# A softmax over the state: DVE's 32x32 block transposes in place of TensorE's

## Chip, cores and metric

The kernel runs on one core of one Trainium2 chip. The metric is the device time of one execution in microseconds, median of the runs. Engines are named as in the profile: PE (TensorE), DVE (VectorE), ACT (ScalarE), POOL (GpSimd), SP (the queue that issues the DMAs).

## What is computed

An attention of 512 tokens and 32 state rows in both directions for 4 batches and 8 heads of width 64, and behind it two feed-forward layers over all 2,176 rows:

```python
scores = scale * x @ state.T            # 512 x 32 for each batch and head
a = softmax(scores, axis=-1)            # over the 32 state rows
xread = a @ state
a2 = softmax(scores.T, axis=-1)         # over the 512 tokens
sread = a2 @ x
h = concat([xread, sread]) as rows of 512
h = prelu(h @ w_in, alpha) @ w_out      # 512 -> 2048 -> 512
out = softplus(h @ moe2_w_in) @ moe2_w_out
```

The change is in `a`, the softmax over the state.

## The kernel before, in words

Every large product is made of three fp32r matmuls (`mm3`, lines 140 to 142): a tile is split into a high half (`split`, line 146, on ACT) and a low half (line 149, on DVE or POOL), and high x high, low x high and high x low are added in PSUM. The weights come as 8-byte words and are converted tile by tile (`wconv`): ACT runs lines 206 and 207, DVE lines 208 to 210, POOL line 211, and the names `exp` and `top` are one buffer each. `wprep` converts and splits the next tile.

The attention works in eight groups: group i holds batch i // 2 and four of its heads. `at_load_t` brings x transposed into scratch tiles t[0] and t[1], `at_load_x` brings x as it is into t[2] and t[3]. Three sets of six scratch tiles take turns, so group 3 uses group 0's (t[0] is acc_94, t[1] is acc_95). For a group:

- `at_scores` (lines 265 to 279) multiplies state by x into one PSUM bank: on the partitions 4 heads x 32 state rows, along the free axis 512 tokens. ACT copies it to t[4] (line 274), DVE takes the maximum (275), ACT takes exp with its sum into t[5] (277).
- `at_rows` (281 to 296) transposes t[4] by four PE transposes of 128x128 (line 287) into another bank, so that tokens lie on the partitions and 16 runs of 32 state rows along the free axis. DVE takes the maximum of each run (290) and subtracts it on the way to t[1] (291), ACT takes exp (292), DVE sums (293) and inverts, POOL multiplies (296).
- `at_back` (298 to 304) transposes t[1] back by four more PE transposes (303) into a bank and splits it into the tiles `at` (high on ACT, low on DVE).
- `at_read` (306 to 334) makes `sread` from t[5], and uses t[0] for a small tile on the way; ACT's line 334 copies its result out of PSUM.

`sw_batch` (line 242) multiplies state by the first layer's weights, so that `hidden` of the first layer multiplies `at` by `sw`. `hidden` (line 348) makes a hidden block in a bank, `act` applies the activation (lines 379 and 383 in the first layer), `out_part` multiplies by the second weights with a lag of three blocks.

PSUM has two pools of four banks, `psa` and `psb`. `pool_s` (line 450) gives the attention's banks from the two in turns, counted over its calls, for the first five groups, and from `psa` after that; `hidden` and `sw_batch` take from `psa`. A bank is given out again when its last reader is done.

Two things set the order of the work. The strings BEFORE and AMONG (lines 47 and 48) set the order in which the steps are written: s, r, d and b are the scores, rows, read and back of a group, x and y its loads, c and p conversions, w a `sw_batch`. A scheduler then sets the order on each engine's queue from its own model of the durations; on the chip each queue runs in that order. Tiles that the order below names pa_... and pb_... are banks.

Of the kernel before, what the change touches and what calls it, by code (L numbers as in the profile page):

```python
# [14 lines left out]
AF = mybir.ActivationFunctionType  # L15
# [43 lines left out]
def mixer_kernel(  # L59
# [200 lines left out]
    def scratch(i):  # L260
        for x in sets[i % 3]:
            held.pop(x.name, None)
        return [x.f for x in sets[i % 3]]

    def at_scores(i):

        b, g = i // 2, i % 2
        t, n2 = scratch(i), st_n[i % 3]
        ps = bank(pool_s(i))
        for k in range(2):  # L270
            for hh in range(2):
                r, o = slice(hh * D, (hh + 1) * D), col(g, k, hh)
                nc.tensor.matmul(ps[o : o + NS], stf.f[r, head(2 * g + k, b)], t[k][r], start=True, stop=True)  # L273
        nc.scalar.activation(t[4], ps, AF.Copy)
        nc.vector.tensor_reduce(out=n2[:, 0:1], in_=ps, op=ALU.max, axis=AX.X)
        nc.vector.tensor_scalar(n2[:, 0:1], n2[:, 0:1], -SCALE, None, op0=ALU.mult)
        nc.scalar.activation(t[5], ps, AF.Exp, bias=n2[:, 0:1], scale=SCALE, accum_out=n2[:, 1:2])
        nc.vector.tensor_scalar(n2[:, 1:2], n2[:, 1:2], EPS, None, op0=ALU.add)
        nc.vector.reciprocal(n2[:, 1:2], n2[:, 1:2])

    def at_rows(i):

        s0, e1 = scratch(i)[4], scratch(i)[1]
        m1, s1 = st_m[i % 2], st_s[i % 2]
        ps = bank(pool_s(i))
        for c in range(4):
            nc.tensor.transpose(ps[:, c * P : (c + 1) * P], s0[:, c * P : (c + 1) * P], ident)
        p3 = ps.rearrange("p (a n) -> p a n", n=NS)
        e3 = e1.rearrange("p (a n) -> p a n", n=NS)
        nc.vector.tensor_reduce(out=m1, in_=p3, op=ALU.max, axis=AX.X)  # L290
        nc.vector.tensor_tensor(out=e3, in0=p3, in1=m1.to_broadcast([P, 16, NS]), op=ALU.subtract)
        nc.scalar.activation(e1, e1, AF.Exp, scale=SCALE)
        nc.vector.tensor_reduce(out=s1, in_=e3, op=ALU.add, axis=AX.X)
        nc.vector.tensor_scalar(s1, s1, EPS, None, op0=ALU.add)
# [2 lines left out]

    def at_back(i):

        e1 = scratch(i)[1]  # L300
        ps = bank(pool_s(i))
        for c in range(4):
            nc.tensor.transpose(ps[:, c * P : (c + 1) * P], e1[:, c * P : (c + 1) * P], ident)
        split(nc.scalar, nc.vector, *R(at[i // 2][i % 2]), ps)

    def at_read(i):

# [250 lines left out]
```

## Time and profile before

| | before |
|---|---|
| median of three runs | 748.48 us (747.7 to 748.65) |
| profiled execution | 746.91 us |
| its span in the trace | 745.1 us |
| PE busy | 722.4 us, 97% |
| DVE busy | 425.2 us, 57% |
| ACT busy | 423.5 us, 57% |
| POOL busy | 170.8 us, 23% |
| DMA, mean over the span | 63 GB/s |

The span is the time between the first and the last instruction on the core; the profiled execution's own time has 1.8 us around it. Busy time is the time in which an engine has an instruction under way. PE overlaps its matmuls, and their ends are modelled, so a full PE is one that always has something to do, not one at its peak. The attention takes up the first 110 us or so, and runs there beside the first layer's first weights.

### The profile page before, as it was taken

What the parts mean: (1) busy time and instruction counts of PE and PEld (TensorE: products, weight loads), DVE (VectorE), ACT (ScalarE), POOL (GpSimd) and SP (SyncE); (2) the same over time, 40 slices, a digit from 0 to 9 for tenths busy, and PEclk for the clock granted to TensorE, in tenths of its full rate; (3) what the DMA queues carried; (4) which work ended last, traced back from release to release, by engine and by line L of the source; (5) the groups of instructions that cost most, each with busy time, mean ns of one, the idle gap of its engine ahead of it and who ended that gap; (6) DMA issues with size and microseconds to landing.
All of it is one profiled execution on the core that took longest, in us unless ns stands there. A gap on an engine that the chain in (4) does not pass through costs nothing.

```text
span 745.1 us, 9504 instructions
## 1 busy us (share of the span) xinstructions
PE 722.4 (97%) x3580; PEld 561.6 (75%) x3580; DVE 425.2 (57%) x693; ACT 423.5 (57%) x764; POOL 170.8 (23%) x142
## 2 busy tenths in 40 slices
PE   5699998999999999999999999999999999999997
PEld 2267666777778777878888888888888888888886
DVE  4898657757778456886585224664257342333433
ACT  4778767735564235564677647765466454444560
POOL 2353332412142003462572004410044000000000
PEclk9989999999999999999999999999999999999999
DMA  9654313203211001220123001220010000001102
GB/s 320 224 177 154 104 41 128 86 1 113 85 57 57 0 1 49 93 85 1 40 74 113 0 1 45 97 86 0 1 53 5 1 1 0 1 1 56 57 15 113
DMA packets 16654, 47.27 MB, mean 63 GB/s; under 512 B 2016, under 2 KB 2016, under 8 KB 16608
## 3 DMA queue, kind: packets, MB, share of 16 engines
q1 hardware_dynamic: 16608, 46.66, 18.7%
q8 instruction: 28, 0.46, 0.3%
q14 instruction: 18, 0.15, 0.1%
HBM read 42.20 MB, written 4.46 MB: 63 GB/s over the span
## 4 chain that ended last, share of the span: by engine, by line
PE 95%; DVE 2%; ACT 1%; DMA 1%; issue 0%; POOL 0%; SPq 0%; ACTq 0%
PE pb L140 17%; PE pb L141 17%; PE pb L142 17%; PE pa L140 13%; PE pa L142 12%; PE pa L141 12%; PE pa L242 2%; PE pa L363 2%; PE pa L273 1%; DMA acc<-xt 1%; DVE top L208 1%; PE pa L371 0%; PE pa L312 0%; PE pb L273 0%; ACT exp L206 0%
## 5 line engine op out<-in xcount | busy, mean ns | idle before, releaser
L390 DVE SCALAR_TENSOR_TENSOR pa<-pa,tmp 128x512 f32<-128x512 f32 x68 | 47.4, 697 | 125.7 <-ACT tmp L389 125.7
L387 ACT ACTIVATE tmp<-pa 128x512 f32<-128x512 f32 x68 | 40.6, 597 | 89.2 <-PE pa L142 69.7
L433 DVE TENSOR_TENSOR acc<-pb,acc 128x512 f32<-128x512 f32 x102 | 67.4, 685 | 35.9 <-PE pb L142 35.9
L208 DVE SCALAR_TENSOR_TENSOR top<-stg,top 128x512 uint16<-128x512 uint16 x64 | 53.0, 828 | 47.5 <-ACT top L207 46.9
L211 POOL TENSOR_TENSOR cnv<-top,cnv 128x512 f32<-128x512 bf16 x48 | 56.3, 1174 | 100.6 <-DVE cnv L210 96.8
L383 DVE SCALAR_TENSOR_TENSOR pa<-tmp,rest,pa 128x512 f32<-128x512 f32 (+1 forms) x80 | 53.2, 671 | 25.5 <-ACT tmp L379 25.0
L206 ACT ACTIVATE exp<-stg 128x512 bf16<-128x512 bf16 x64 | 43.0, 672 | 39.6 <-DVE cnv L210 28.9
L379 ACT ACTIVATE tmp<-pa 128x512 f32<-128x512 f32 x68 | 40.2, 597 | 42.2 <-PE pa L142 35.7
L207 ACT ACTIVATE top<-exp,top_bias 128x512 uint16<-128x512 uint16 x64 | 46.2, 722 | 9.3 <-POOL cnv L211 5.7
L389 ACT ACTIVATE tmp<-tmp 128x512 f32<-128x512 f32 x68 | 42.9, 631 | 1.7
L388 ACT ACTIVATE tmp<-tmp 128x512 f32<-128x512 f32 x68 | 42.9, 631 | 1.5
L210 DVE SCALAR_TENSOR_TENSOR cnv<-stg,exp 128x512 f32<-128x512 uint32 x48 | 35.8, 745 | 12.8 <-POOL wo5l L149 4.0
L209 DVE TENSOR_SCALAR exp<-top 128x512 uint16<-128x512 uint16 x64 | 32.2, 503 | 1.1
L146 ACT ACTIVATE g1h<-pa 128x512 fp32r<-128x512 f32 x33 | 19.7, 597 | 20.5 <-DVE pa L390 12.3
L146 ACT ACTIVATE g3h<-pa 128x512 fp32r<-128x512 f32 x33 | 19.7, 597 | 19.4 <-DVE pa L383 9.7
L146 ACT ACTIVATE g0h<-pa 128x512 fp32r<-128x512 f32 x33 | 19.7, 596 | 19.1 <-DVE pa L383 10.2
L149 DVE TENSOR_TENSOR g3l<-pa,g3h 128x512 fp32r<-128x512 f32 x33 | 22.7, 689 | 13.5 <-ACT g3h L146 13.2
L149 DVE TENSOR_TENSOR g1l<-pa,g1h 128x512 fp32r<-128x512 f32 x33 | 22.7, 687 | 12.6 <-ACT g1h L146 12.2
L149 DVE TENSOR_TENSOR g0l<-pa,g0h 128x512 fp32r<-128x512 f32 x33 | 22.7, 688 | 10.5 <-ACT g0h L146 10.1
L149 DVE TENSOR_TENSOR g2l<-pa,g2h 128x512 fp32r<-128x512 f32 x33 | 22.7, 686 | 10.0 <-ACT g2h L146 9.9
L146 ACT ACTIVATE g2h<-pa 128x512 fp32r<-128x512 f32 x33 | 19.8, 599 | 14.5 <-DVE pa L390 7.6
L149 POOL TENSOR_TENSOR wo3l<-cnv,wo3h 128x512 fp32r<-128x512 f32 x5 | 6.5, 1304 | 74.5 <-ACT wo3h L146 74.3
(863 smaller groups left out, 2114.5 us busy)
## 6 DMA issues: line engine op xcount, KB each, us to landing
stg<-w1i SPq DMA_DIRECT2D x16, 511.8 KB, 4.1
stg<-w1o SPq DMA_DIRECT2D x16, 511.8 KB, 3.4
stg<-w2i SPq DMA_DIRECT2D x16, 511.8 KB, 4.0
stg<-w2o SPq DMA_DIRECT2D x16, 511.8 KB, 3.3
out<-acc SPq DMA_DIRECT2D x16, 256.0 KB, 2.0
acc<-xt SPq DMA_DIRECT2D x10, 256.0 KB, 4.5
acc<-xs SPq DMA_DIRECT2D x8, 256.0 KB, 5.1
wo4h<-xt SPq DMA_DIRECT2D x3, 256.0 KB, 3.8
```

Of the source, the lines that this page charges most:

```text
L140: nc.tensor.matmul(ps, lh, rh, start=start, stop=False)
L141: nc.tensor.matmul(ps, lh, rl, start=False, stop=False)
L142: nc.tensor.matmul(ps, ll, rh, start=False, stop=stop)
L146: nc.scalar.activation(h, src, AF.Copy)
L149: eng_l.tensor_tensor(out=l, in0=src, in1=h, op=ALU.subtract)
L206: nc.scalar.activation(e, top.bitcast(BF16), AF.Abs)
L207: nc.scalar.activation(tu, eu, AF.Relu, bias=top_bias, scale=TOP_SCALE)
L208: nc.vector.scalar_tensor_tensor(out=tu, in0=top, scalar=TOP_SIGN, in1=tu, op0=ALU.bitwise_and, op1=ALU.bitwise_or)
L211: nc.gpsimd.tensor_tensor(out=a, in0=t, in1=a, op=ALU.add)
L383: nc.vector.scalar_tensor_tensor(out=ps[:, cs], in0=t[:, cs], scalar=a, in1=ps[:, cs], op0=ALU.mult, op1=ALU.add)
L390: nc.vector.scalar_tensor_tensor(out=ps, in0=ps, scalar=0.0, in1=t, op0=ALU.max, op1=ALU.add)
L433: nc.vector.tensor_tensor(out=a, in0=ps, in1=a, op=ALU.add)
```

## The change

`at_scores` no longer copies its bank to t[4]: DVE transposes it from PSUM to t[1], in blocks of 32x32. A block holds 32 state rows of one head by 32 tokens, so that after it the partitions hold 4 heads x 32 tokens and each run of 32 along the free axis holds the state rows of one token: what the maximum and the sum need. `at_rows` works in t[1]: the maximum on DVE from SBUF, the subtraction on POOL, the rest as before. `at_back` transposes t[1] by DVE into t[0] and splits that: high on ACT, low on POOL. The eight PE transposes of a group and two of its five banks go. The calls that `pool_s` counts are fewer, so the turns between the pools shift.

```diff
--- before.py
+++ after.py
@@ -271,7 +271,7 @@
             for hh in range(2):
                 r, o = slice(hh * D, (hh + 1) * D), col(g, k, hh)
                 nc.tensor.matmul(ps[o : o + NS], stf.f[r, head(2 * g + k, b)], t[k][r], start=True, stop=True)
-        nc.scalar.activation(t[4], ps, AF.Copy)
+        nc.vector.transpose(out=t[1], in_=ps)
         nc.vector.tensor_reduce(out=n2[:, 0:1], in_=ps, op=ALU.max, axis=AX.X)
         nc.vector.tensor_scalar(n2[:, 0:1], n2[:, 0:1], -SCALE, None, op0=ALU.mult)
         nc.scalar.activation(t[5], ps, AF.Exp, bias=n2[:, 0:1], scale=SCALE, accum_out=n2[:, 1:2])
@@ -280,15 +280,11 @@
 
     def at_rows(i):
 
-        s0, e1 = scratch(i)[4], scratch(i)[1]
+        e1 = scratch(i)[1]
         m1, s1 = st_m[i % 2], st_s[i % 2]
-        ps = bank(pool_s(i))
-        for c in range(4):
-            nc.tensor.transpose(ps[:, c * P : (c + 1) * P], s0[:, c * P : (c + 1) * P], ident)
-        p3 = ps.rearrange("p (a n) -> p a n", n=NS)
         e3 = e1.rearrange("p (a n) -> p a n", n=NS)
-        nc.vector.tensor_reduce(out=m1, in_=p3, op=ALU.max, axis=AX.X)
-        nc.vector.tensor_tensor(out=e3, in0=p3, in1=m1.to_broadcast([P, 16, NS]), op=ALU.subtract)
+        nc.vector.tensor_reduce(out=m1, in_=e3, op=ALU.max, axis=AX.X)
+        nc.gpsimd.tensor_tensor(out=e3, in0=e3, in1=m1.to_broadcast([P, 16, NS]), op=ALU.subtract)
         nc.scalar.activation(e1, e1, AF.Exp, scale=SCALE)
         nc.vector.tensor_reduce(out=s1, in_=e3, op=ALU.add, axis=AX.X)
         nc.vector.tensor_scalar(s1, s1, EPS, None, op0=ALU.add)
@@ -297,11 +293,9 @@
 
     def at_back(i):
 
-        e1 = scratch(i)[1]
-        ps = bank(pool_s(i))
-        for c in range(4):
-            nc.tensor.transpose(ps[:, c * P : (c + 1) * P], e1[:, c * P : (c + 1) * P], ident)
-        split(nc.scalar, nc.vector, *R(at[i // 2][i % 2]), ps)
+        t = scratch(i)
+        nc.vector.transpose(out=t[0], in_=t[1])
+        split(nc.scalar, nc.gpsimd, *R(at[i // 2][i % 2]), t[0])
 
     def at_read(i):
 
```

Since the scheduler sets the queues anew, the change also moves instructions. (Lines of the new kernel are smaller by 4 to 6 from `at_rows` on: its L287 is the subtraction, its L292 is the old L296, its L306, L312 and L322 are the old L312, L318 and L328.)

POOL, from its first weight tile on, before:

```order
L211 TENSOR_TENSOR wi0h<-top_74,wi0h 128x512
L211 TENSOR_TENSOR wi0l<-top_74,wi0l 128x512
L296 TENSOR_TENSOR acc_95<-acc_95,sts_81 128x512
L211 TENSOR_TENSOR wi1h<-top_74,wi1h 128x512
L296 TENSOR_TENSOR wo4l<-wo4l,sts_82 128x512
L211 TENSOR_TENSOR wi1l<-top_74,wi1l 128x512
L211 TENSOR_TENSOR cnv_67<-top_74,cnv_67 128x512
L149 TENSOR_TENSOR wo0l<-cnv_67,wo0h 128x512
```

Between wi0h's and wi1l's conversions stand two others and the multiplications of groups 0 and 1. With the change the same stretch of POOL's queue holds:

```order
L211 TENSOR_TENSOR wi0h<-top_74,wi0h 128x512
L287 TENSOR_TENSOR acc_95<-acc_95,stm_79 128x512
L211 TENSOR_TENSOR wi0l<-top_74,wi0l 128x512
L287 TENSOR_TENSOR wo4l<-wo4l,stm_80 128x512
L292 TENSOR_TENSOR acc_95<-acc_95,sts_81 128x512
L211 TENSOR_TENSOR wi1h<-top_74,wi1h 128x512
L292 TENSOR_TENSOR wo4l<-wo4l,sts_82 128x512
L287 TENSOR_TENSOR acc_101<-acc_101,stm_79 128x512
L149 TENSOR_TENSOR at0l<-acc_94,at0h 128x512
L211 TENSOR_TENSOR wi1l<-top_74,wi1l 128x512
L292 TENSOR_TENSOR acc_101<-acc_101,sts_81 128x512
L149 TENSOR_TENSOR at1l<-wo4h,at1h 128x512
```

The subtractions of groups 0, 1 and 2 (L287) and the low half at0l (L149) now stand in front of wi1l's conversion, and at1l two places behind it.

SP, the reloads of the first scratch set, before:

```order
L258 DMA acc_96<-xs 128x512
L258 DMA acc_97<-xs 128x512
L254 DMA acc_95<-xt 128x512
L192 DMA stg_66<-w1o 128x2047
L254 DMA acc_94<-xt 128x512
L258 DMA wo5h<-xs 128x512
```

Here the two loads of group 3 (acc_95, acc_94) stand between weight tiles. With the change the same stretch of SP's queue holds:

```order
L258 DMA acc_96<-xs 128x512
L258 DMA acc_97<-xs 128x512
L192 DMA stg_66<-w1o 128x2047
L258 DMA wo5h<-xs 128x512
L258 DMA wo5l<-xs 128x512
L254 DMA acc_95<-xt 128x512
L192 DMA stg_64<-w1o 128x2047
L254 DMA acc_94<-xt 128x512
L254 DMA wo4l<-xt 128x512
```

The loads of group 3 into acc_95 and acc_94 have moved behind two weight tiles and behind the loads of wo5h and wo5l. What was read last from acc_94 was at_read's small tile; now it is the split in `at_back`.

PE, around the first matmul of `hidden` (at0h by sw0h), before:

```order
L312 MATMUL pa_464<-ident,at7l 128x128 x4
L287 MATMUL pa_493<-ident,acc_98 128x128 x4
L140 MATMUL pa_514<-at0h,sw0h 128x512
L141 MATMUL pa_514<-at0l,sw0h 128x512
L142 MATMUL pa_514<-at0h,sw0l 128x512
L140 MATMUL pa_514<-at1h,sw1h 128x512
L141 MATMUL pa_514<-at1l,sw1h 128x512
L142 MATMUL pa_514<-at1h,sw1l 128x512
L312 MATMUL pa_534<-ident,acc_99 128x128 x4
L318 MATMUL pb_470<-acc_102,wi4l 32x64 x8
L318 MATMUL pb_470<-wi4h,wi4l 32x64 x8
```

Group 3's transposes stand directly ahead of the first `hidden` matmul, and group 2's read behind its set of six. With the change the same place on PE's queue holds:

```order
L242 MATMUL pa_416<-wi0l,ex0h 32x512
L242 MATMUL pa_417<-wi1l,ex0h 32x512
L312 MATMUL pa_447<-acc_102,wi4l 32x64 x8
L312 MATMUL pa_447<-wi4h,wi4l 32x64 x8
L140 MATMUL pa_482<-at0h,sw0h 128x512
L141 MATMUL pa_482<-at0l,sw0h 128x512
L142 MATMUL pa_482<-at0h,sw0l 128x512
L140 MATMUL pa_482<-at1h,sw1h 128x512
L141 MATMUL pa_482<-at1l,sw1h 128x512
L142 MATMUL pa_482<-at1h,sw1l 128x512
L306 MATMUL pb_502<-ident,acc_99 128x128 x4
L273 MATMUL pb_531<-wo4h,ex0h 32x512 x2
L273 MATMUL pb_531<-wo4l,ex0h 32x512 x2
```

The transposes of group 3's rows (L287) are gone from the front, and the 32 small matmuls of group 2's read (the old L318) have come to stand ahead of the first `hidden` matmul.

## Rows read from the trace of the kernel before

**Rows 1.** The page, part 1: busy time, share of the span, instructions.
```profile
PE 722.4 (97%) x3580; PEld 561.6 (75%) x3580; DVE 425.2 (57%) x693; ACT 423.5 (57%) x764; POOL 170.8 (23%) x142
```

**Rows 2.** Engines by stretch: from:to, length, PE, PEld, DVE, ACT, POOL busy, clock, DMA.
```profile
0.00:36.00 36.00, 20.70 (x167) 7.99 (x168) 23.29 (x53) 22.10 (x47) 11.00 (x15) 0.98 0.78 271
36.00:72.00 36.00, 35.86 (x294) 23.93 (x293) 33.29 (x67) 28.68 (x65) 15.41 (x14) 0.92 0.50 162
72.00:92.00 20.00, 20.00 (x132) 13.46 (x131) 14.47 (x30) 14.77 (x35) 4.93 (x5) 1.00 0.41 130
```

**Rows 3.** PE's waits, 35 to 200 us: us in total, times, longest.
```profile
PE pa L140 <- DVE g1l L149: 2.4, 1, 2.4
PE pa L140 <- DVE stn L276: 1.4, 1, 1.4
PE pa L140 <- ACT srh L334: 1.2, 1, 1.2
```

**Rows 4.** Chain that ended last, 35 to 103 us: start, length in us, what.
```profile
35.43 0.78 PE pa L140
...
43.44 0.44 PE pb L303 x4
...
89.81 0.58 PE pa L318 x32
...
92.51 0.59 ACT at6h L146
...
93.81 0.29 ACT srh L334 x2
...
102.53 0.44 PE pa L303 x4
```

**Rows 5.** Engines in stretches of 4 us; columns as in group 2 (clock behind POOL).
```profile
32.00:36.00 4.00, 1.87 (x9) 1.34 (x10) 4.00 (x11) 2.84 (x7) 1.25 (x2) 0.84 0.07 13
36.00:40.00 4.00, 4.00 (x42) 3.04 (x40) 3.88 (x10) 3.83 (x8) 2.31 (x3) 0.50 0.36 123
40.00:44.00 4.00, 4.00 (x34) 1.91 (x26) 3.96 (x8) 2.56 (x6) 2.09 (x3) 0.81 0.63 195
```

**Rows 6.** Groups, 0 to 180 us (last row: whole span): busy us, mean ns, idle before.
```profile
L291 DVE TENSOR_TENSOR acc<-pa,stm 128x512 f32<-128x512 f32 x4 | 2.7, 680 | 0.0
...
L293 DVE TENSOR_REDUCE sts<-acc 128x16 f32<-128x512 f32 x5 | 3.4, 679 | 0.0
...
L296 POOL TENSOR_TENSOR wo4l<-wo4l,sts 128x512 f32<-128x512 f32 x3 | 3.1, 1049 | 6.6 <-ACT g1h L146 5.2 <-DVE sts L295 1.4
...
L149 POOL TENSOR_TENSOR wo3l<-cnv,wo3h 128x512 fp32r<-128x512 f32 x5 | 6.5, 1304 | 74.5 <-ACT wo3h L146 74.3
```

**Rows 7.** L208 and L209, 0 to 180 us: as groups, and as minimum/median/maximum in ns.
```profile
L208 DVE SCALAR_TENSOR_TENSOR top<-stg,top 128x512 uint16<-128x512 uint16 x28 | 22.4, 801 | 20.8 <-ACT top L207 20.5
...
L209 DVE TENSOR_SCALAR exp<-top 128x512 uint16<-128x512 uint16 x28 | 9.8, 349 | 0.5
...
L208 DVE SCALAR_TENSOR_TENSOR top<-stg,top x28: 673/692/1507, 7.9 to 177.0; 128x512 uint16<-128x512 uint16 x28
...
L209 DVE TENSOR_SCALAR exp<-top x28: 276/291/1286, 8.6 to 178.2; 128x512 uint16<-128x512 uint16 x28
```

**Rows 8.** Instructions in order of time at 21.5 us: start, length, engine, what.
```profile
21.55 1.05 POOL L296 TENSOR_TENSOR wo4l<-wo4l,sts 128x512 f32<-128x512 f32 x1 [0.49 <-DVE sts L295]
...
21.85 1.29 DVE L208 SCALAR_TENSOR_TENSOR top<-stg,top 128x512 uint16<-128x512 uint16 x1 [0.47 <-ACT top L207]
```

**Rows 9.** wi1l on POOL; DMA issue (KB, us to landing); scores on the chain; L277.
```profile
24.75 1.16 POOL L211 TENSOR_TENSOR wi1l<-top,wi1l 128x512 f32<-128x512 bf16 x1 [2.15 <-DVE wi1l L210]
...
acc<-xt SPq DMA_DIRECT2D x10, 256.0 KB, 4.5
...
14.40 1.00 PE pa L273 x4
...
L277 ACT ACTIVATE acc<-pb,stn x2: 677/682/687, 11.3 to 35.8; 128x512 f32<-128x512 f32 x2
```

## Prediction

> **What bounds the kernel now.** I read the page's busy times first, then the engines by stretch, then TensorE's waits, then the chain that ended last. The page gives TensorE (PE) 97% of the span, VectorE (DVE) and ScalarE (ACT) 57% each and GpSimd (POOL) 23% [rows 1]. The stretches show that this average hides stages [rows 2]. Up to 36 us PE is busy 20.7 of 36 us: it waits for loads and for the other engines. From 36 us on it is full. From 36 to 72 us DVE is nearly full too (33.3 of 36 us, so 2.7 us idle), and from 72 us on DVE has a quarter of its time free. After 35 us PE waits only three times, 5.0 us in all [rows 3]; the first of these is in front of the first matmul of `hidden`, which starts at 35.43 us [rows 4]. So after 35.43 us what PE no longer has to do comes off the end, unless PE then waits for somebody. Before it, only the moment of that first matmul counts. One more thing lies in the start: after PE was busy 1.9 of 4 us, the granted clock falls to 0.50, the lower level of 1.2 GHz, and is still on its way back between 40 and 44 us [rows 5].
>
> **PE.** The order shows both transposing steps gone, 64 instructions in 16 groups of four. Seven of the groups stand on the chain behind 35.43 us, the first at 43.44 and the last at 102.53 us, with 0.44 us each [rows 4]: **3.1 us saved**. The rest run ahead of 35.43 us, where PE has idle time, or beside waits; I count nothing for them. The order also puts the 32 small matmuls of group 2's read in front of the first `hidden` matmul; such a set costs 0.58 us at full clock [rows 4]: **0.6 us saved** behind it.
>
> **The wait at 92 us.** There PE waits 1.2 us for a bank that ACT's L334 copies free [rows 3], and just ahead of that copy ACT splits what the transposes of group 6 left in PSUM [rows 4]. The new at_back takes no bank. I take the wait as gone: **1.2 us saved**; bounds 0 and the 3.6 us of both later waits.
>
> **DVE.** A group loses the subtraction (L291, 0.68 us) and the low half of the split from PSUM, and gains two transposes, which no row of before shows. The nearest rows are DVE's other passes over 128x512 of fp32: 0.68 us from PSUM (L291) and from SBUF (L293) [rows 6]. I take 0.69, so that the exchange costs nothing. The bounds are the cheapest and the dearest 128x512 pass of DVE, 0.28 us (16-bit data) and 1.51 us [rows 7]. By the Trainium skill, "VectorE: DVE Perf Modes", section "The three transpose paths", a 128x128 bf16 transpose takes 311 ns on DVE and 390 ns on TensorE; scaled to four such widths, an estimate from that page, one of ours would take 1.24 us on DVE, and the sum would come out 6.6 us higher. DVE's price no run here shows; on PE the trace has four transposes in 0.44 us, far less than the page.
>
> **ACT** loses eight copies (L274), which are off the path.
>
> **POOL** takes over the subtraction, in the form of L296 (1.05 us), and the low half, in the form of L149 (1.30 us) [rows 6]. That is 8 x 2.35 = 18.8 us more, and POOL was busy 26.4 of the first 72 us [rows 2]: there is room, but not at once. Two things follow.
>
> The first is a hindrance of DVE. A DVE pass of the weight conversion that starts while POOL works on two fp32 tensors is held: L208, 0.69 us alone, took 1.29 us when L296 had begun 0.30 us earlier [rows 8]. Over the first 180 us L208 averages 0.801 us for a median of 0.692, and L209 0.349 for 0.291, 28 times each [rows 7]: 28 x (0.109 + 0.058) = 4.7 us lost, with 19 such POOL passes there (8 of L296, 11 of L149): 0.25 us each. The Trainium skill, "GPSIMD Engine Reference", section "8. Key points", says that POOL shares its SBUF interfaces with DVE and contends with DVE passes in a 2-port mode or with two SBUF inputs. By that rule, and by the 1.29 us, this speaks against the change.
>
> The second is the queue. In front of the conversion of wi1l, the last tile that sw_batch needs, POOL's order has three subtractions and one low half more: 3 x 1.05 + 1.30 = 4.5 us. Most of it lies where POOL waited, but at0l stands directly in front.
>
> **The first matmul of `hidden`.** It uses the bank of group 3's scores, and these need a reload of acc_94, which now must wait for at0l on POOL. wi1l's conversion started at 24.75 us [rows 9]; I put at0l's end at 25.6, 0.9 us behind that. The reload lands 4.5 us after its issue [rows 9]: 30.1. Then come the scores 1.0 (L273) [rows 9], a transpose and two maxima, 3 x 0.69, a pass of L208, 0.69, and the exponential, 0.68 [rows 9]: 34.5. With two of the hold-ups of 0.6 us [rows 8] and some 0.7 us for small passes and hand-overs (an estimate) it is 36.4 us: **1.0 us lost**. Bounds: 2 us earlier (no hold-up, the reload early) and 3 us later. The slow clock takes half of PE's rate from 35.43 to 40 us and a fifth up to 44 us, some 3 us in all [rows 5]; I keep it as it is, and it may go or double.
>
> **DVE between 36 and 72 us.** Ten of the added POOL passes fall there: 10 x 0.25 = 2.5 us more for DVE, while PE has six groups less, 2.6 us. Against 2.7 us of idle time DVE could come up to 2.4 us late; past 72 us it has time to catch up. I take **1.0 us lost**, bounds 0 and 2.4.
>
> **Sum:** -3.1 - 0.6 - 1.2 + 1.0 + 1.0 = **-2.9 us**. The profiled execution took 746.91 us (the span of 745.1 and 1.8 us around it), so it would take 744.0. The median of the runs is 748.48 us, 1.6 above it: the forecast in those terms is **745.6 us**. About 0.2% (1.5 us) is what a measurement here can tell from no change.
>
> **Rivals.**
> 1. *Fewer banks, fewer waits.* Two bank uses a group go. If the 2.4 us wait for DVE's g1l [rows 3] and the 1.0 us of DVE's lateness go as well, the time is 745.6 - 3.4 = 742.2. For it: both late waits are for banks. Against: the second hangs on a split of DVE that stays.
> 2. *The transposes are dear and DVE becomes the bound: slower.* Six transposes stand ahead of the first `hidden` matmul and about six between there and 72 us, where DVE is the tighter engine. Each 0.1 us above 0.69 costs 1.2 us. If a transpose takes as long as a held L208, 1.29 us [rows 8], the time is 745.6 + 12 x 0.60 = 752.8; it is slower than before from 0.93 us on. For it: DVE's 33.3 of 36 us [rows 2]. Against: DVE's fp32 passes of this size show 0.68 us whatever they do. The page's 1.24 us, named above, would give 752.2.
> 3. *POOL's queue gives the gain back.* at0l, the subtractions and the conversions queue behind one another, and the first `hidden` matmul comes 3.5 us later instead of 1.0: 748.1, no change. For it: 18.8 us more on an in-order queue. Against: POOL is busy 11.0 of the first 36 us [rows 2].
> 4. *The change doesn't do what it says*: excluded by the order, which has 16 transposes on DVE and 64 fewer on PE.
>
> **How the numbers follow.** Forecast 0.51, rival 1 0.14, rival 2 0.18, rival 3 0.17. Faster by over 0.2% (below 747.0): rival 1 and most of the forecast (0.44), 0.58. Same: the rest of the forecast and most of rival 3, 0.21. Slower (above 750.0): rival 2 and a little of rival 3, 0.21. The forecast's own range is 743 to 748. To hold 8 in 10 the range takes in rival 1 with some of the clock's 3 us beyond it, and on the other side rival 3 and the nearer half of rival 2: **740.5 to 751.5 us**.
>
> **What would show it.** Right: the first `hidden` matmul at about 36.4 us; transposes of 0.65 to 0.75 us; longer means of L208 and L209 (0.9 and 0.4 us); no PE wait at 92 us. Wrong: transposes above 0.93 us; PE waits of several us for POOL (at0l, at1l, wo0l); the first matmul later than 38 us; a slow clock that lasts past 48 us.

## The result, and the profile after

The changed kernel takes **757.52 us** (median of four runs, 756.47 to 757.77), against 748.18 us for the kernel before on the same chip: 1.0122 times as long, 95% interval 1.0105 to 1.014. The forecast was 745.6 us, in a range of 740.5 to 751.5. The profiled execution took 756.47 us with a span of 754.7 us, 9.6 us more than before. Two executions among the experiments below, of 1,867.64 and 4,108.85 us, stand outside all medians here.

The page's busy times, and the first line of its chain of waits:

```profile
PE 720.7 (96%) x3516; PEld 557.5 (74%) x3516; DVE 435.3 (58%) x693; ACT 421.4 (56%) x756; POOL 192.5 (26%) x158
...
PE 86%; DVE 7%; ACT 3%; issue 2%; DMA 1%; POOL 0%; SPq 0%; DVEq 0%; ACTq 0%
```

PE has the 64 transposes less [rows 1], and is busy no longer than before; yet the span grew. So PE waited more. The engines by stretch say where (from:to, length, busy time of PE, PEld, DVE, ACT and POOL, clock, DMA):

```profile
0.00:36.00 36.00, 20.37 (x173) 6.82 (x174) 26.73 (x52) 19.74 (x40) 18.00 (x20) 0.87 0.78 270
36.00:72.00 36.00, 29.33 (x204) 18.21 (x196) 30.61 (x56) 24.89 (x55) 21.69 (x18) 0.94 0.46 139
72.00:92.00 20.00, 16.53 (x108) 10.61 (x101) 15.63 (x28) 12.02 (x30) 7.22 (x6) 0.91 0.42 140
```

From 36 to 72 us PE was full before, 35.86 of 36 us [rows 2]; now it is busy 29.33. From 72 to 92 us it falls from 20.0 to 16.53. DVE, which I had feared would be the tighter engine there, is busy *less* than before between 36 and 72 us (30.61 for 33.29): it is not full. PE's waits from 30 to 180 us name what it stood for (us in total, times, longest):

```profile
PE pa L312 <- ACT acc L307: 2.9, 1, 2.9
PE pa L312 <- ACT wo6h L307: 2.5, 1, 2.5
PE pa L140 <- DVE sw2l L149: 2.3, 1, 2.3
PE pb L140 <- ACT g0h L146: 2.1, 1, 2.1
PE pb L140 <- ACT g1h L146: 1.8, 1, 1.8
PE pa L140 <- ACT acc L277: 1.3, 1, 1.3
PE pa L273 <- DMA acc<-xt: 1.0, 1, 1.0
PE pb L140 <- ACT g2h L146: 0.8, 1, 0.8
PE pa L306 <- DVE g0l L149: 0.5, 1, 0.5
PE pb L141 <- DVE g1l L149: 0.4, 1, 0.4
```

Where before had three waits [rows 3], there are now nine behind the first `hidden` matmul and at it. The row for L277 is the first `hidden` matmul's own wait, at 37.59 us, and the DMA's 1.0 us lies ahead of it. The other eight sum to 13.3 us; before, the two behind the first matmul were 3.6 [rows 3]. The two longest are L312, the small matmuls of a read, waiting for L307, ACT's copy of that read's transposes.

**Where the 9.6 us come from.** The first `hidden` matmul starts at 37.59 instead of 35.41 us: +2.2. The waits behind it: +9.7. The granted clock falls to 0.50 twice more, behind two of the waits:

```profile
82.00:84.00 2.00, 2.00 (x6) 1.61 (x5) 1.53 (x3) 0.36 (x1) 0.32 (x2) 0.50 0.22 81
106.00:108.00 2.00, 2.00 (x6) 1.61 (x6) 0.69 (x1) 1.13 (x3) 0.79 (x1) 0.50 0.00 0
80.00:86.00 6.00, 5.60 (x46) 3.81 (x46) 3.50 (x6) 1.78 (x4) 2.71 (x3) 0.72 0.46 146
104.00:110.00 6.00, 5.35 (x16) 3.92 (x16) 2.38 (x4) 3.10 (x10) 1.53 (x2) 0.72 0.02 9
```

Over each 6 us the mean is 0.72, which loses 6 x 0.28 = 1.7 us: +3.4 for both. Not every wait is followed by a dip: behind the two longest, at 45 and 69 us, the granted clock stayed at 1.00. The dip in the start [rows 5] comes earlier now, 28 to 40 us, so that less of it lies behind the first `hidden` matmul: 1.5 us instead of 3.0 by the same sum over 2 us pieces, -1.5. Against this stands PE's saved work: ten of the groups of transposes stood behind the first `hidden` matmul before, 10 x 0.44 us, and group 2's read, 0.6: -5.0. Together 2.2 + 9.7 + 3.4 - 1.5 - 5.0 = +8.8, of the 9.6 measured.

**The first `hidden` matmul.** The chain that ended last, from DVE's conversion of wi1l through the reload of acc_94 to that matmul (start, length in us, what), and the low half at0l on POOL, behind which the prediction had put the reload:

```profile
24.79 1.02 DVE exp L209
...
25.87 1.62 DVE wi1l L210
27.54 0.33 SPq L192
...
27.96 3.57 DMA acc<-xt
...
31.67 1.08 PE pa L273 x4
...
33.66 0.72 DVE acc L274
...
34.87 0.67 DVE stm L286
35.54 1.05 DVE top L208
...
36.75 0.78 ACT acc L277 x2
```

```profile
25.62 1.31 POOL L149 TENSOR_TENSOR at0l<-acc,at0h 128x512 fp32r<-128x512 f32 x1
```

From the reload on it runs through the steps that the prediction named. Ahead of the reload it does not: at0l was done at 26.93 us, but the reload was issued only at 27.96, because the load of a weight tile (L192) stands ahead of it in SP's queue and waited for DVE's L210 on wi1l. Three held passes of DVE lie on this chain: L209 of 1.02 us, L210 of 1.62 and L208 of 1.05, where they take 0.29, 0.69 and 0.69 alone, some 2 us of hold together.

**A wait of 2.9 us, in its making.** The instructions in order of time behind 40 us, those that bear on it (start, length in us, engine, what, in brackets the idle time before it and who ended it):

```profile
40.33 1.05 POOL L292 TENSOR_TENSOR acc<-acc,sts 128x512 f32<-128x512 f32 x1 [0.70 <-ACT wo1h L146]
40.93 0.99 DVE L208 SCALAR_TENSOR_TENSOR top<-stg,top 128x512 uint16<-128x512 uint16 x1 [0.20 <-ACT top L207]
41.34 1.71 POOL L149 TENSOR_TENSOR wo1l<-cnv,wo1h 128x512 fp32r<-128x512 f32 x1
41.96 1.24 DVE L209 TENSOR_SCALAR exp<-top 128x512 uint16<-128x512 uint16 x1
43.23 0.69 DVE L210 SCALAR_TENSOR_TENSOR cnv<-stg,exp 128x512 f32<-128x512 uint32 x1
43.96 0.66 ACT L206 ACTIVATE exp<-stg 128x512 bf16<-128x512 bf16 x1 [2.31 <-DVE cnv L210]
...
44.52 0.58 ACT L307 ACTIVATE acc<-pb 128x512 f32<-128x512 f32 x1
...
45.16 0.65 PE L312 MATMUL pa<-acc,acc 128*32 128x64 f32 x32 [2.91 <-ACT acc L307]
```

POOL runs two fp32 passes back to back. DVE's L208 takes 0.99 us beside them for 0.69, and L209 1.24 for 0.29. ACT's next conversion, L206, waits 2.31 us for DVE; the copy L307, which needs nothing from DVE, stands behind L206 in ACT's queue; and PE's L312 waits 2.91 us for the copy. The two holds come to 0.30 + 0.95 = 1.25 us, so that by these rows PE would wait some 1.7 us even without them (an estimate): the place of the copy behind L206 counts as much as the lateness. PE's own queue there, from its order, with group 3's transposes and the matmuls that use their copy:

```
L306 MATMUL pb_502<-ident,acc_99 128x128 x4
L273 MATMUL pb_531<-wo4h,ex0h 32x512 x2
L273 MATMUL pb_531<-wo4l,ex0h 32x512 x2
L322 MATMUL pa_447<-ident,acc_100 128x128
L312 MATMUL pa_508<-acc_96,acc_98 32x64 x8
```

Between transposes and result stand only four score matmuls and one transpose. For group 4 it is tighter still: its L312 stands directly behind its L306, and waits 2.5 us. There ACT had its wait for DVE earlier (1.84 us, up to 64.25 us) and is busy without a gap from then on; when the transposes are done, at 66.7 us, it still has three L425 (from 66.50 us) and L207 in front of the copy, which starts at 68.55.

The new operations themselves are close to their forecast (forms of a line over 0 to 180 us: busy us, mean ns | idle before):

```profile
L208 DVE SCALAR_TENSOR_TENSOR top<-stg,top 128x512 uint16<-128x512 uint16 x26 | 21.7, 833 | 16.9 <-ACT top L207 16.8
L209 DVE TENSOR_SCALAR exp<-top 128x512 uint16<-128x512 uint16 x26 | 14.3, 551 | 0.5
L287 POOL TENSOR_TENSOR acc<-acc,stm 128x512 f32<-128x512 f32 x5 | 6.8, 1361 | 10.1 <-PE pa L306 4.5 <-DVE stn L276 3.1 <-DVE stm L286 2.5
...
L297 DVE STREAM_TRANSPOSE acc<-acc 128x512 f32<-128x512 f32 x5 | 3.4, 687 | 0.0
...
L274 DVE STREAM_TRANSPOSE acc<-pa 128x512 f32<-128x512 f32 x3 | 2.1, 711 | 0.3 <-PE pa L273 0.3
```

A transpose takes 0.69 to 0.71 us. The subtraction takes 1.05 us at the least and 1.36 on the mean of these five. L209 averages 0.551 us (0.349 before [rows 7]).

### The profile page after: what moved, and what is told of

Its sections match the earlier page's. It is cut to its first block, busy times and chain, and to the rows that moved or that the text cites. A ratio compares the mean times of both kernels' runs of the same rounds, so it can differ in the third digit from the quotient of the medians.

```text
span 754.7 us, 9368 instructions
## 1 busy us (share of the span) xinstructions
PE 720.7 (96%) x3516; PEld 557.5 (74%) x3516; DVE 435.3 (58%) x693; ACT 421.4 (56%) x756; POOL 192.5 (26%) x158
## 4 chain that ended last, share of the span: by engine, by line
PE 86%; DVE 7%; ACT 3%; issue 2%; DMA 1%; POOL 0%; SPq 0%; DVEq 0%; ACTq 0%
PE pb L141 16%; PE pb L142 16%; PE pb L140 15%; PE pa L140 12%; PE pa L142 12%; PE pa L141 12%; PE pa L357 2%; PE pa L242 2%; DMA acc<-xt 1%; DVE top L208 1%; DVE exp L209 1%; ACT exp L206 1%; ACT acc L425 1%; DVE stn L275 1%; DVE pa L377 1%
## 5 line engine op out<-in xcount | busy, mean ns | idle before, releaser
L208 DVE SCALAR_TENSOR_TENSOR top<-stg,top 128x512 uint16<-128x512 uint16 x64 | 53.7, 839 | 45.8 <-ACT top L207 45.3
L206 ACT ACTIVATE exp<-stg 128x512 bf16<-128x512 bf16 x64 | 43.0, 672 | 47.9 <-DVE cnv L210 33.5
L207 ACT ACTIVATE top<-exp,top_bias 128x512 uint16<-128x512 uint16 x64 | 46.1, 720 | 10.2 <-POOL cnv L211 5.7
L210 DVE SCALAR_TENSOR_TENSOR cnv<-stg,exp 128x512 f32<-128x512 uint32 x48 | 36.6, 763 | 12.9 <-POOL wo5l L149 4.0
L209 DVE TENSOR_SCALAR exp<-top 128x512 uint16<-128x512 uint16 x64 | 37.4, 584 | 1.2
L149 DVE TENSOR_TENSOR g3l<-pa,g3h 128x512 fp32r<-128x512 f32 x33 | 22.7, 688 | 14.2 <-ACT g3h L146 14.0
L149 DVE TENSOR_TENSOR g0l<-pa,g0h 128x512 fp32r<-128x512 f32 x33 | 22.7, 688 | 11.4 <-ACT g0h L146 11.1
L149 DVE TENSOR_TENSOR g1l<-pa,g1h 128x512 fp32r<-128x512 f32 x33 | 22.6, 685 | 11.6 <-ACT g1h L146 11.2
L149 DVE TENSOR_TENSOR g2l<-pa,g2h 128x512 fp32r<-128x512 f32 x33 | 22.6, 686 | 11.4 <-ACT g2h L146 11.2
L149 POOL TENSOR_TENSOR wo3l<-cnv,wo3h 128x512 fp32r<-128x512 f32 x5 | 6.9, 1373 | 74.0 <-ACT wo3h L146 73.9
```

Of the source, the lines that this page charges most:

```text
L149: eng_l.tensor_tensor(out=l, in0=src, in1=h, op=ALU.subtract)
L206: nc.scalar.activation(e, top.bitcast(BF16), AF.Abs)
L207: nc.scalar.activation(tu, eu, AF.Relu, bias=top_bias, scale=TOP_SCALE)
L208: nc.vector.scalar_tensor_tensor(out=tu, in0=top, scalar=TOP_SIGN, in1=tu, op0=ALU.bitwise_and, op1=ALU.bitwise_or)
```

## The experiments

The theories, by short names:
- **HOLD**: DVE's passes are held beside POOL's added fp32 passes, DVE is late, and all that hangs on DVE with it.
- **QUEUE**: the subtraction and the low half stand in POOL's queue in front of what others wait for.
- **TURNS**: `pool_s` counts fewer calls, so the banks are dealt out differently. By program order, the results of the reads of groups 1 to 4 have moved from `psb` to `psa` (their transposes the other way), the scores of group 3 from `psb` to `psa` and those of group 4 back. `hidden` and `sw_batch` draw from `psa` too.
- **ORDER**: the scheduler's order for this one kernel is unlucky, whatever the reason; the next one would be better. (The expectations written first count the new turns under ORDER; later ones call it SCHEDULE, or the rival.)

"Held time" below is the sum, over all DVE passes from 0 to 140 us, of what a pass took beyond its line's median plus 0.1 us: before 4.3 us, after 11.5. All ratios are to the kernel before on the same chip, whose median was 747.8 to 748.3 us in each of the comparisons.

| run | median us | ratio (95%) | first `hidden` us | held us |
|---|---|---|---|---|
| before | 748.2 | 1 | 35.4 | 4.3 |
| after | 757.5 | 1.0122 (1.0105 to 1.014) | 37.6 | 11.5 |
| turns_as_before | 740.7 | 0.9918 (0.9902 to 0.9934) | 32.7 | 11.1 |
| both_on_dve | 748.3 | 1.0008 (0.9996 to 1.0019) | 36.5 | 6.9 |
| subtract_on_dve | 749.0 | 1.0022 (1.0009 to 1.0036) | 35.7 | 11.8 |
| low_on_dve | 749.8 | 1.0038 (1.0024 to 1.0052) | 35.0 | 8.4 |
| before_with_pool_passes | 748.8 | 1.0008 (0.9996 to 1.002) | 35.7 | 5.8 |
| forward_only | 751.4 | 1.004 (1.0025 to 1.0054) | 36.1 | 6.8 |
| back_only | 743.1 | 0.9937 (0.9921 to 0.9954) | 36.2 | 8.4 |
| shared_maximum | 748.4 | 1.0003 (0.999 to 1.0016) | 35.0 | 8.9 |
| before_with_new_turns | 749.5 | 1.0026 (1.0015 to 1.0037) | 37.0 | 4.7 |
| read_results_in_psb | 745.6 | 0.9976 (0.996 to 0.9992) | 36.3 | 14.0 |
| scores3_in_psb | 749.7 | 1.0031 (1.0019 to 1.0043) | 37.3 | 11.0 |
| shared_maximum_old_turns | 739.7 | 0.9902 (0.988 to 0.9924) | 31.3 | 12.2 |
| order_with_new_turns | 754.5 | 1.0091 (1.0076 to 1.0106) | 37.4 | 10.5 |
| order_with_old_turns | 744.4 | 0.9954 (0.9939 to 0.9968) | 32.2 | 14.0 |
| results_written_later | 750.0 | 1.0033 (1.0023 to 1.0044) | 37.3 | 11.3 |

**1. The parts on POOL.** Three kernels take work off POOL again, in the changed kernel:

```diff
# subtract_on_dve; both_on_dve has both edits
-        nc.gpsimd.tensor_tensor(out=e3, in0=e3, in1=m1.to_broadcast([P, 16, NS]), op=ALU.subtract)
+        nc.vector.tensor_tensor(out=e3, in0=e3, in1=m1.to_broadcast([P, 16, NS]), op=ALU.subtract)
# low_on_dve
-        split(nc.scalar, nc.gpsimd, *R(at[i // 2][i % 2]), t[0])
+        split(nc.scalar, nc.vector, *R(at[i // 2][i % 2]), t[0])
```

> The changed kernel with the subtraction alone back on DVE; the low half stays on POOL. HOLD is weakened by the kernel before with POOL passes, which lost nothing. QUEUE, sharpened: what costs is the subtraction on POOL, because the exponential, the sum and the rest of a group wait for it in POOL's queue, while the low half is needed late. Then this kernel is near the one with only the transposing back changed: 742 to 748 us. ORDER (whatever the scheduler happens to make of it): anything from 743 to 758. HOLD: eight POOL passes less and eight DVE passes more: 754 to 758.

> The changed kernel with the low half alone back on DVE; the subtraction stays on POOL. QUEUE, sharpened: the loss stays, 752 to 758 us. ORDER: anything from 743 to 758. HOLD: 754 to 758.

> The changed kernel with the subtraction and the low half back on DVE; the transposes stay DVE's. Three theories for the 9.3 us. HOLD: the added POOL passes over two fp32 tensors hold DVE passes (about 0.44 us each, 7.1 us more than before up to 140 us) where DVE is nearly full, and PE waits for DVE. Then DVE loses 7 us of holds but gains 16 passes of 0.68 = 10.9 us: 757 to 761 us, no better than the change. QUEUE: the groups come late because their steps stand in POOL's in-order queue with passes of 1.05 to 1.3 us: then 745 to 750 us. ORDER: the scheduler's new order and the new turns of the banks do it, whichever engine has the passes: 754 to 760 us, and with waits of PE at the same places.

Measured: 749.0, 749.8 and 748.3 us. Each of the two, taken off POOL alone, gives back 8 us, and both together give back 9: the parts don't add. So neither is "the" cause: taking away either one removes most of the loss. For both_on_dve only QUEUE's range held, for low_on_dve only ORDER's, which excludes little, and for subtract_on_dve ORDER's again. Held time doesn't order these runs either: subtract_on_dve has 11.8 us of it, more than after, and is 8.5 us faster.

**2. POOL's passes without the rest.** Two idle fp32 passes a group on POOL in the kernel before, on scratch that nobody reads any more:

```diff
         nc.vector.tensor_tensor(out=e3, in0=p3, in1=m1.to_broadcast([P, 16, NS]), op=ALU.subtract)
+        nc.gpsimd.tensor_tensor(out=s0, in0=s0, in1=s0, op=ALU.subtract)
...
         split(nc.scalar, nc.vector, *R(at[i // 2][i % 2]), ps)
+        nc.gpsimd.tensor_tensor(out=e1, in0=e1, in1=e1, op=ALU.subtract)
```

> The kernel before, with PE's transposes and DVE's subtraction and low half, and two additional POOL passes over two fp32 tensors a group in the places where the change has them; nobody needs their results, and what they compute reaches no output. HOLD: L208, L209 and L210 show some 7 us of holds up to 140 us and the time rises by 4 to 8 us: 752 to 756. QUEUE: nobody waits for these results, so only the conversions behind them come later: 748 to 751. ORDER: banks and PE's steps are those of before: 747 to 750.

Measured: 748.8 us, no change. The held time rose to 5.8 us only, not to 11.5, so this run does not copy the whole of HOLD; it shows that sixteen passes of POOL as such cost the kernel before nothing.

**3. One half of the change at a time.** forward_only transposes forward on DVE with the subtraction on POOL, and goes back by PE as before; back_only is the reverse. In both, the two ways of transposing lay the rows out differently, so that values of the output stand in wrong places; only the time is read.

```diff
# forward_only, in at_back
-        nc.vector.transpose(out=t[0], in_=t[1])
-        split(nc.scalar, nc.gpsimd, *R(at[i // 2][i % 2]), t[0])
+        e1 = scratch(i)[1]
+        ps = bank(pool_s(i))
+        for c in range(4):
+            nc.tensor.transpose(ps[:, c * P : (c + 1) * P], e1[:, c * P : (c + 1) * P], ident)
+        split(nc.scalar, nc.vector, *R(at[i // 2][i % 2]), ps)
```

> Only the transposing in front of the softmax on DVE, with the subtraction on POOL; the transposing back on PE and the low half on DVE, as before. HOLD: eight POOL passes more, DVE's work as in the change: half of the holds and half of PE's saving: 751 to 754 us. QUEUE: the subtraction stands in the path of each group: 751 to 755. ORDER: anything between 746 and 758, not halfway.

> Only the transposing behind the softmax on DVE, with the low half on POOL; scores, rows and subtraction as before. HOLD: eight POOL passes more: 751 to 754 us. QUEUE: the low half is needed late (the second matmul of a set), so less: 747 to 751. ORDER: anything between 746 and 758; the two halves need not add up to 9.3 us.

Measured: 751.4 and 743.1 us. The halves are 3.1 us slower and 5.2 us faster than before (748.29), together -2.1; the whole is +9.3. back_only lies below the range of every theory. Each half has a deal of the banks of its own (in both, the reads have their results half in `psa`, half in `psb`, but the scores of group 3 are in `psa` in forward_only and in `psb` in back_only), so these two runs mix parts and turns, and can't separate them.

**4. No subtraction at all.** shared_maximum takes one maximum per partition and gives it to ACT's exp as a bias.

```diff
-        nc.vector.tensor_reduce(out=m1, in_=e3, op=ALU.max, axis=AX.X)
-        nc.gpsimd.tensor_tensor(out=e3, in0=e3, in1=m1.to_broadcast([P, 16, NS]), op=ALU.subtract)
-        nc.scalar.activation(e1, e1, AF.Exp, scale=SCALE)
+        nc.vector.tensor_reduce(out=m1[:, 0:1], in_=e1, op=ALU.max, axis=AX.X)
+        nc.vector.tensor_scalar(m1[:, 0:1], m1[:, 0:1], -SCALE, None, op0=ALU.mult)
+        nc.scalar.activation(e1, e1, AF.Exp, bias=m1[:, 0:1], scale=SCALE)
```

> The changed kernel without a subtraction pass: one maximum over a partition's 16 runs in place of 16, taken off by ACT's exponential as its bias (the softmax is the same, only the shift is shared by 16 tokens). The low half stays on POOL. QUEUE: the subtraction leaves the path altogether and DVE has less work than with subtract_on_dve: 740 to 746 us, below both kernels. HOLD: eight POOL passes less: 749 to 754. ORDER: anything from 741 to 757.

Measured: 748.4 us. Eight POOL passes fewer give back 9 us, as much as run 1's; with the new turns it still only draws level with the kernel before. QUEUE had expected 740 to 746, HOLD 749 to 754.

**5. The turns of before.** Two lines make `pool_s` count as it did:

```diff
         e1 = scratch(i)[1]
+        nps[0] += 1
         m1, s1 = st_m[i % 2], st_s[i % 2]
...
         t = scratch(i)
+        nps[0] += 1
         nc.vector.transpose(out=t[0], in_=t[1])
```

> The changed kernel with the count that gives the banks in turns moved on in rows and back as before, so that every scores and read step takes its banks from the same pool as before. QUEUE and HOLD: no difference from the change, 755 to 760 us. ORDER by way of the banks (scores in psa, whose banks hidden needs): half or more of the loss gone, 747 to 753.

Measured: **740.7 us**, 16.8 us less than the changed kernel (whose kernel before took 748.18 us, 747.93 here) and 7.3 less than before. That lies below every expected range; ORDER by way of the banks had the direction. The instructions on every engine are the same in number, and the held time is nearly the same (11.1 for 11.5 us). PE's waits of this run from 30 to 180 us, and the stretch from 36 to 72 us (columns as above):

```profile
PE pa L140 <- DVE sw2l L149: 2.1, 1, 2.1
PE pa L141 <- DMA wo4l<-xt: 0.9, 1, 0.9
PE pa L140 <- ACT at1h L146: 0.8, 1, 0.8
PE pa L314 <- ACT wo6h L309: 0.8, 1, 0.8
PE pb L140 <- ACT g0h L146: 0.7, 1, 0.7
PE pa L140 <- DVE g0l L149: 0.5, 1, 0.5
PE pa L308 <- ACT acc L277: 0.3, 1, 0.3
PE pa L308 <- ACT at7l L277: 0.2, 1, 0.2
```

```profile
36.00:72.00 36.00, 35.66 (x284) 22.43 (x285) 33.66 (x70) 28.33 (x63) 24.80 (x20) 0.91 0.47 153
```

PE is full again, 35.66 of 36 us. The first `hidden` matmul starts at 32.65 us. The scores of group 3 lie in `psb`, and it waits for DVE's split of a `sw_batch` (sw2l) instead; their place alone does not make it early, as scores3_in_psb (run 7) shows with 37.25 us. The row of 2.1 us is its own wait and that of 0.2 us lies ahead of it; the rest, 4.0 us, compares with 13.3 of the changed kernel. So 4.9 us of the 15.4 between the spans are the earlier start and 9.3 the waits; the clock's two later dips are gone too. Why L314 (the reads' matmuls, L312 above) hardly waits, two queues show, PE's and ACT's (its copy is L309 here):

```
L308 MATMUL pa_502<-ident,acc_99 128x128 x4
L273 MATMUL pa_531<-wo4h,ex0h 32x512 x2
L273 MATMUL pa_531<-wo4l,ex0h 32x512 x2
L140 MATMUL pa_544<-at0h,sw0h 128x512
...
L142 MATMUL pa_544<-at1h,sw1l 128x512
L324 MATMUL pb_447<-ident,acc_100 128x128
L314 MATMUL pb_508<-acc_96,acc_98 32x64 x8
```

```profile
39.64 0.59 ACT L309 ACTIVATE acc<-pa 128x512 f32<-128x512 f32 x1
40.23 0.68 ACT L206 ACTIVATE exp<-stg 128x512 bf16<-128x512 bf16 x1
```

Six matmuls of `hidden` now stand between group 3's transposes and its result, and for group 4 some forty rows do, where the changed kernel had none. And group 3's copy now stands ahead of the conversion L206 in ACT's queue, not behind it: it is done at 40.23 us, where the changed kernel's began at 44.52. So with the old turns the scheduler has moved the copy as well as its user.

**6. The turns alone, in the kernel before.** Each step's pool is written out, with the pools that the changed kernel gives to scores and reads; the steps' code stays.

```diff
-        ps = bank(pool_s(i))
+        ps = bank(pool_s(f"d{i}T"))
...
-    def pool_s(i):
-        nps[0] += 1
-        return psb if (i < 5 and nps[0] % 2) else psa
+    IN_PSB = "s0 r0 d0T b0 d1T s2 d2T b2 d3T s4 b3 d4T b4".split()
+
+    def pool_s(step):
+        return psb if step in IN_PSB else psa
```

(s is a group's scores, r and b its rows and back, dT and dO the transposes and the result of its read.)

> The kernel before, in which each scores and read step takes its banks from the pools that the change gives it (its own rows and back steps keep theirs). TURNS: what cost the change its gain is that the read results of groups 1 to 4 and the scores of group 3 came into psa, whose banks hidden and sw_batch need; then the kernel before loses by it too, without any transposing on DVE: 752 to 762 us, with waits of PE between 40 and 130 us. Rival SCHEDULE (the good result with the old turns is a lucky order of one program): 746 to 751 us.

Measured: 749.5 us, 0.26% more than before. The expectation of TURNS missed: by themselves the new turns cost the old kernel about 2 us, not 4 to 14. So what makes them dear is something in the change itself; that it is DVE's lateness, and ACT's through it, fits the waits shown above, but no run shows it separately.

**7. Which bank it is.** The changed kernel with the results of the reads in `psb` (and their transposes in `psa`, for group 0 too), and with only the scores of group 3 in `psb`:

```diff
# read_results_in_psb
+    IN_PSB = "s0 d0O d1O s2 d2O d3O s4 d4O".split()
# scores3_in_psb; the changed kernel's own list is this one without s3
+    IN_PSB = "s0 d0T d1T s2 s3 d2T d3T s4 d4T".split()
```

> The changed kernel with its own turns for the scores, but for groups 0 to 4 the read's transposes in psa and the read's results in psb. TURNS: the results' banks are held longest, from PE's small matmuls to ACT's last copy, so most of the loss goes: 741 to 748 us. SCHEDULE: 749 to 758 us, or anything.

> The changed kernel with one bank moved: the scores of group 3, on which the first hidden matmul waited, in psb. TURNS: the first hidden matmul comes 1 to 4 us earlier, the later waits stay: 752 to 757 us. SCHEDULE: anything between 745 and 760 us.

Measured: 745.6 and 749.7 us: 11.9 and 7.8 us off the changed kernel's time. Again the two don't add to the 16.8 of both. In scores3_in_psb the first `hidden` matmul hardly came earlier (37.25 us), so that part of what was expected missed, and the time with it (752 to 757 us): the gain lies in the waits behind it. Moving the reads' banks is the larger part: with them in `psb` no L312 waits for L307 behind 36 us, though the held time rises to 14.0 us.

**8. The turns or a lucky order.** Undoing anything at all had given back 6 us or more, which is what ORDER would say. So three neighbours of the written order were exchanged, under either deal of the banks, each step's pool written out so that the exchange moves none:

```diff
-BEFORE = "... x4 s3 w1 c0"
+BEFORE = "... x4 s3 c0 w1"
-AMONG = ("d2 r3 b2", "d3 s4 x5", "b3", "r4", "s5 y5 p0 d4 x6", ...
+AMONG = ("d2 r3 b2", "s4 d3 x5", "b3", "r4", "d4 s5 y5 p0 x6", ...
```

> The changed kernel with its own turns of the banks, each step's pool written out, and three neighbours in the written order exchanged: the scores of group 4 ahead of the read of group 3, the read of group 4 ahead of the scores of group 5, the last conversion ahead of the last sw_batch of the start. Some 330 rows of TensorE's queue move, no bank changes its pool. Theory (the loss belongs to the turns: read results and scores 3 in psa): 753 to 760 us, as the changed kernel's 757.5. Rival (it belongs to one unlucky order of the queues, and other orders scatter by several us): 742 to 750 us.

> The same exchange of three neighbours in the changed kernel with the turns of before (740.7 us unexchanged). Theory: 738 to 744 us. Rival (luck of the order): 746 us or more.

Measured: 754.5 and 744.4 us. The exchange moves one kernel by -3.0 and the other by +3.7 us (in order_with_old_turns a wait of 3.1 us for `g0h` behind 100 us is new). So this one exchange is good for 3 or 4 us either way, and the turns still set the two 10 us apart. order_with_old_turns lies 0.4 us outside what TURNS expected, and 1.6 short of ORDER's 746.

**9. The matmuls that waited, moved.** The new turns stay; the reads of groups 2 to 4 are written in two parts, transposes and copy (t) where the read stood, the result (o) a step later.

```diff
-AMONG = ("d2 r3 b2", "d3 s4 x5", "b3", "r4", "s5 y5 p0 d4 x6", "p0 r5 s6", ...
+AMONG = ("t2 r3 o2 b2", "t3 s4 x5", "o3 b3", "r4", "s5 y5 p0 t4 x6", "o4 p0 r5 s6", ...
```

> The changed kernel with its own turns; the reads of groups 2, 3 and 4 are cut in two in the written order, the transposes with their copy where they stood and the 32 small matmuls with what follows one step later (group 2: behind its neighbour's rows). No bank changes its pool. Theory (the results stand in front of PE's queue too close behind ACT's copy, which comes late): the waits of 2.9 and 2.5 us of L312 for L307 go, and a dip of the clock or two of 2.1 us each with them: 748 to 752 us. Rival (the late ACT copy shows up in the next matmul of hidden, which waits for a bank): 755 to 759 us, with the waits at L140 longer by as much.

Measured: 750.0 us, inside what was expected. The same stretch behind 43 us:

```profile
43.70 0.66 ACT L206 ACTIVATE exp<-stg 128x512 bf16<-128x512 bf16 x1 [2.36 <-DVE cnv L210]
44.27 0.58 ACT L307 ACTIVATE acc<-pb 128x512 f32<-128x512 f32 x1
...
44.90 0.65 PE L317 MATMUL pa<-acc,acc 128*32 128x64 f32 x32 [1.25 <-ACT acc L307]
```

ACT waits as long for DVE (2.36 us for 2.31) and the copy comes as late (44.27 for 44.52), but PE has six matmuls of `hidden` in front of the result (L317 here) and waits 1.25 us instead of 2.91; the wait for `wo6h` is gone, and so are the clock's dips at 82 and 106 us (which stood behind PE's waits for `g1h` and `g0h`, and not, as was expected, behind the waits for L307). The first `hidden` matmul stays at 37.3 us.

**10. The best of both.** shared_maximum with the turns of before:

```diff
+    IN_PSB = "s0 d0T d1O s2 s3 d2O d3O d4O".split()
```

> The kernel with the shared maximum (no subtraction pass, the shift common to a partition's 16 tokens) and the turns of before. TURNS: the loss by the banks goes, and DVE and POOL have less to do than in the change with the old turns (740.7): 735 to 741 us. SCHEDULE: 740 to 750 us.

Measured: 739.7 us, 0.9902 (0.988 to 0.9924) of before. It beats both kernels; against turns_as_before the intervals overlap, so the shared maximum adds nothing that these runs can tell. Three pairs of changed kernels now differ in the deal of the banks alone, with the same steps in the same written order: 757.5 and 740.7 us, 754.5 and 744.4, 748.4 and 739.7. The deal is worth 16.8, 10.1 and 8.6 us in them, so the 16.8 of run 5 is the largest of three. All the changed kernels with exactly the new deal took 748 us or more, all with the old one 744.4 or less.

## Why the prediction was wrong

**What held.** The transposes: 0.69 us forecast, 0.69 to 0.71 measured; with that rival 2 falls. The estimate of 1.24 us from the Trainium skill's page "VectorE: DVE Perf Modes", section "The three transpose paths", is not borne out by this trace for fp32 in 32x32 blocks. PE's saved work: 3.7 us forecast, 5.0 by the rows, because ten groups and not seven stood behind the first `hidden` matmul. Group 2's read did move ahead of that matmul. The wait for `srh` at 92 us is gone as said. The kernel with the old turns is faster than before, as the sum said of the change, but its 740.7 us do not confirm the sum: they lie 4.9 us below it, and the first `hidden` matmul there comes 2.8 us earlier than before, where the sum had it 1.0 later.

**What was off in size.** The first `hidden` matmul: 36.4 us forecast, 37.59 measured. at0l began at 25.62 us, where I had its end, and took 1.31. But the reload did not wait for it: it was issued 1.0 us after at0l's end, behind a weight tile's load that waited in SP's queue for DVE's L210, itself held to 1.62 us. It took 3.6 us for the 4.5 forecast and landed at 31.53 instead of 30.1; the rest followed. So the bank of group 3's scores was the right place, and the release of the reload the wrong one. The price of an added POOL pass on DVE: 0.25 us forecast, (11.5 - 4.3) / 16 = 0.45 measured, over 0 to 140 us (by different sums: the forecast's took L208 and L209 alone). Between 36 and 72 us, though, only five of the added passes ran and not ten, and the held time there rose by 1.3 us, from 3.2 to 4.5, not by 2.5. So the amount of hold in that stretch was less than forecast, and the loss is not made of it. The slow clock, kept at 3 us by the sum, came to 4.9 behind the first `hidden` matmul (1.5 and 3.4). The Trainium skill's page "GPSIMD Engine Reference", section "8. Key points", says that POOL contends with DVE instructions in a 2-port mode or with two SBUF inputs. The trace agrees for L208, which has two SBUF inputs and took 0.99 us for 0.69; for L209, which has one and took 1.24 for 0.29, no trace shows the mode.

**The step that failed.** It is what the sum had for PE's waits behind the first `hidden` matmul: the 1.2 us saved at 92 us ("The new at_back takes no bank. I take the wait as gone.") and the 1.0 us lost by DVE's lateness, together -0.2 us. These waits grew by 9.7 us, from 3.6 to 13.3. I counted banks, as fewer and so as a gain, and stopped there. That the turns shift was known beforehand, and the sum has the scores of group 3 as a bank that the first `hidden` matmul needs; I did not write out which pool the reads draw from afterwards. Two of the shifts matter: the scores of group 3 and the reads' results move into `psa`, where `hidden` and `sw_batch` draw. The runs show what that does: with the old deal the same change gains 7.3 us, with the new one it loses 9.3, and moving the reads' banks alone takes 11.9 us off.

**The step that let it through.** "DVE could come up to 2.4 us late" took lateness as an amount of time that DVE owes at the end of the stretch, and set it against DVE's idle time. But in the wait followed above PE doesn't wait for DVE at the end of a stretch. It waits for one copy on ACT that stands behind one conversion that waits for two held passes, and how much of that reaches PE depends on how many matmuls stand in between on PE's own queue. Experiment 9 shows it: the same late copy costs 2.91 us with a transpose and four matmuls in between, 1.25 us with six more. The order of PE after the change shows L312 directly behind L306 for group 4; that could have been read beforehand, and so could the place of the copy in ACT's queue.

**Rivals.** Rival 1 (fewer banks, fewer waits) has the right place and the wrong sign under the new turns; under the old ones the time goes below its 742.2. Rival 3 (POOL's queue) was a loss at the first `hidden` matmul: that came 2.2 us later, not 3.5, and the chain ahead of it runs through DVE's held conversions and SP's queue; no PE wait behind it is for POOL. None of the rivals was what happened: new waits behind the first matmul under the new turns, 5.4 us of them for ACT's copies of the reads' transposes.

**What stays open.** Of the 13.3 us of waits, the 2.9 us one is followed back step by step and the 2.5 us one to a busy ACT; the other six, 7.9 us, are not. That the scheduler puts a read's result so close behind its copy *because* of the pool its bank comes from, and a copy behind a conversion, is argued from the two orders, not shown separately; the scheduler's order couldn't be held fixed while the pools change. Nor do the single parts add up (runs 1, 3, 4 and 7): with three or four microseconds from any change of the order, differences of that size between two of these kernels are not to be explained one by one.

## What to carry to other kernels

Where resources are dealt out in turns by a counter, a change that drops some of the calls deals all the rest anew. Write out who gets what before and after, and time the change with the old deal first: here that was two lines and 16.8 us (8.6 and 10.1 in two more pairs). And a copy that comes late costs what is missing between its producer and its user on the waiting engine's queue, not what the average slack of the engines says; read that distance, and what stands ahead of the copy on its own queue, from the order for each user that the change moves.

## What the runs showed of the hardware

- A small pass of DVE can be held as long as a large one. L290, 128x16 elements, takes 0.17 us by itself; it took 1.15 us when POOL's L149 had begun 0.16 us earlier:

```profile
79.21 1.28 POOL L149 TENSOR_TENSOR at4l<-wo4h,at4h 128x512 fp32r<-128x512 f32 x1 [0.44 <-ACT at4h L146]
79.37 1.15 DVE L290 TENSOR_SCALAR sts<-sts 128x16 f32<-128x16 f32 x1
...
102.08 0.17 DVE L290 TENSOR_SCALAR sts<-sts 128x16 f32<-128x16 f32 x1
```

- POOL's passes vary as well: in the attention the subtraction takes from 1.05 to 1.52 us and L149 from 1.27 to 1.73. DVE was at work beside short and long ones alike; what decides which of the two engines is slowed, these rows don't show.
- Two of PE's waits, 1.8 and 2.1 us long, were followed by a fall of the granted clock to 0.50 (1.2 GHz) at 82 and at 106 us, which cost another 1.7 us each time. Two longer ones, 2.9 and 2.5 us, were not: the clock stayed at 1.00 behind them. So a wait can cost more than its length, and its length alone does not say whether it will.
